# A gated linear attention with a feed-forward block on one core: element work leaves GpSimd, the recurrent state becomes block-diagonal, and the program is put in a new order

## The chip, the core and the metric

The kernel runs on 1 core of one Trainium2 chip. The core has five engines that run their own instruction queues strictly in order and meet only at semaphores: TensorE (PE, matrix multiply, with PEld for its weight loads), VectorE (DVE), ScalarE (ACT), GpSimd (POOL) and SyncE (SP, which here only starts DMAs). The metric is device time in microseconds (us) of the whole program; lower is better. The kernel before takes 174.16 us, the median of 3 runs (172.9 to 175.22).

## The reference: what is computed

```python
batch, n_heads, seq, head_dim = (4, 8, 768, 48)      # r, k, v, w; u is (8, 48)
for t in range(S):
    cur   = einsum('bhd,bhe->bhde', u * k[t], v[t])
    y[t]  = einsum('bhd,bhde->bhe', r[t], state + cur)
    state = w[t][..., None] * state + einsum('bhd,bhe->bhde', k[t], v[t])
x = y.transpose(0, 2, 1, 3).reshape(3072, 384)
out = ((x @ w1) * (x @ w2)) @ w3 @ w_out              # w1, w2: 384 x 1024; w3: 1024 x 1024; w_out: 1024 x 384
```

The first part is a recurrence over 768 steps for 32 pairs of batch and head, with a 48 x 48 state each and a decay w per channel. The second part is a feed-forward block on 3072 tokens.

## The kernel before

**Chunks and units.** The sequence is cut into 6 chunks of 128 steps. Within a chunk the recurrence is done by matrix products: with the running sum of log w over the chunk, r is scaled up and k scaled down, so that the strictly causal part of (r k^T) is one product with a mask, and the state enters once per chunk. A *unit* is one chunk of one or two batches. There are 13 units, numbered 0 to 12: units 0 and 1 have one batch, all others two. In the words below "the ninth unit" is unit 8, and so on.

**The steps of a unit t**, with the names that the program's order uses:
- `win_t`, `kin_t`, `rin_t`, `vin_t`: the loads. All but one are issued by GpSimd. A DMA from GpSimd waits on one of eight semaphores in turn, so that at most eight are under way.
- `ln_t` (ScalarE): log w. `cs_t` (PE): its running sum by a triangular matrix. `ne_t`, `e_t`, `iw_t`, `pc_t` (ScalarE): the exponentials.
- `KRk_t`, `rw_t`, `KRr_t` (VectorE): scaled k and r. `trk_t`, `trr_t` (PE) transpose them through the identity, eight transposes each for a unit of two batches, and `trke_t`, `trre_t` copy them out of PSUM. For units in `DMA_K` and `DMA_R` the DMAs `dtk_t`, `dtr_t` on SP's queue do this instead.
- `m_t_b` (PE): the product r k^T of batch b, 8 heads. `msk_t_b` (VectorE, out of PSUM) applies the causal mask; for the second batch of units 5 to 12 ScalarE copies (`mcp`) and GpSimd applies the mask in place (`maff`).
- `rk_t`, `ruk_t`, `dg_t` (VectorE): the diagonal term with u; `dv_t` multiplies it with v, on GpSimd in nine of 13 units.
- `y_t` (PE): for each head the state times r (L684, a product of 64 rows by 48 columns) and the masked product times v (L690). `yb_t` (VectorE) adds `dv` and writes y.
- `yt_t`, `xT_t`: transposes of y on PE and a copy; for units in `DMA_Y` the DMAs `dty_t_0`, `dty_t_1` on SP's queue.
- `kv_t` (PE), `T_t` (VectorE), `S_t`, `Sb_t`: the new state, its decay and its copy in bf16. `S_t` is on GpSimd in eight units.

**The feed-forward block** of a unit: `a_t_g`, `b_t_g` (PE, L786) are x w1 and x w2, for units of two batches in four groups g of six matmuls each; `asb_t_g` copies a out of PSUM, `abT_t_g` (VectorE, L796) multiplies it with b; `o_t_b` (PE, L802, eight matmuls) is the product with w34; `osb_t_b` copies and `st_t_b` (SP) stores. w34 = w3 w_out is computed once at the start (`wt_`, `w3Te_`, `wm_`, `w34e_`), while the first units run.

**What sets the order.** No scheduler decides. The string `ORDER` lists every step with its engine, `name@engine`, and the program issues the steps in that order; each engine's queue is that list cut down to the engine. `PLACES` gives every step its buffer and its PSUM bank. An entry `warm7@15` issues 15 matmuls on zeros (L373) that keep TensorE busy and compute nothing.

Of the kernel before, what the change touches and what calls it, by code (L numbers as in the profile page):

```python
# [102 lines left out]
et_1@ACT warm1@3 wm_3_0@PE win_2@POOL ne_1@ACT ne_0@ACT wm_6_0@PE ucast@ACT w3_4@POOL wm_7_0@PE warm1@1 wm_7_1@PE
vin_0@POOL wm_2_0@PE w34e_7@DVE vin_1@POOL wm_2_1@PE KRk_1@DVE kin_2@POOL umm@PE KRk_0@DVE trr_1@PE trr_0@PE ucp@ACT
KRr_1@DVE wm_6_1@PE pc_0@ACT w34e_2@ACT rk_1@DVE rin_2@POOL ruk_1@DVE wt_0_0@PE trk_0@PE rk_0@DVE wt_1_0@PE ruk_0@DVE
trk_1@PE w34e_6@DVE wm_3_1@PE win_3@POOL trke_1@ACT KRr_0@DVE wt_1_1@PE trke_0@ACT wt_0_1@PE w3Te_1_0@DVE m_1_0@PE
# [756 lines left out]
```

## Time and profile before

| | |
|---|---|
| median of 3 runs | 174.16 us (172.9 to 175.22) |
| the profiled execution | 173.97 us, its span (first to last instruction) 172.3 us |
| so outside the span | 1.67 us |
| busy share of the span | PE 93%, DVE 77%, ACT 55%, POOL 57% |
| mean granted TensorE clock | 0.988 |
| last matmul ends, and the span after it | 168.2 us, 4.1 us |

A line of the timeline reads: start, length, engine, source line, operation, output and inputs, count, and in brackets how long the engine was idle before it and who released it. In the windows the columns behind the stretch are its length and then the busy time of PE, PEld, DVE, ACT and POOL with the number of instructions, the granted clock, the DMA load and the bytes moved. Times of y_t in what follows are the ends of its last matmuls (L690): y_3 46.95, y_4 60.32, y_5 77.51, y_9 117.16, y_12 145.09 us.

### The profile page before, as it was taken

The numbers are of one execution on the slowest core, as the hardware profiler recorded it, in microseconds if no ns is written. First come the engines' busy times: TensorE is split into PE (matmuls) and PEld (weight loads), VectorE is DVE, ScalarE is ACT, GpSimd is POOL, SyncE is SP. The second block draws the span as 40 slices with busy tenths as digits, with TensorE's granted clock in tenths as the row PEclk, the third lists the DMA queues.
The fourth block names the chain that finished last, engine by engine and source line by source line (L and its number), as shares of the span: only waits on it lengthen the run. The fifth ranks groups of instructions, "written<-read, shape, count | busy, mean of one in ns | idle before, by whom it ended". The sixth has DMA issues, their size and how long they took to land.

```text
span 172.3 us, 4685 instructions
## 1 busy us (share of the span) xinstructions
PE 160.0 (93%) x1956; PEld 119.6 (69%) x1956; DVE 133.2 (77%) x222; ACT 94.1 (55%) x161; POOL 97.8 (57%) x99
## 2 busy tenths in 40 slices
PE   5889999989999999599999999989989899999990
PEld 2364658558897789357778878667767687886750
DVE  4022798989889999969999899997988745856660
ACT  2125387867568699449888769855661430110301
POOL 7975968699988879694599972040057520000000
PEclk9999999999999999969999999999999999999999
DMA  4999999999999999999999999547879803400333
GB/s 70 159 200 171 235 178 189 177 184 163 170 196 175 163 161 197 175 160 205 71 61 234 119 68 157 111 125 158 166 154 111 142 12 83 137 0 4 137 137 139
DMA packets 98663, 24.36 MB, mean 141 GB/s; under 512 B 88833, under 2 KB 97026, under 8 KB 98642
## 3 DMA queue, kind: packets, MB, share of 16 engines
q0 software_dynamic: 81536, 16.06, 107.9%
q1 hardware_dynamic: 17106, 8.00, 18.9%
q8 instruction: 15, 0.25, 0.6%
q14 instruction: 6, 0.05, 0.1%
HBM read 27.79 MB, written 4.72 MB: 189 GB/s over the span
## 4 chain that ended last, share of the span: by engine, by line
PE 54%; DMA 17%; DVE 13%; ACT 5%; POOL 3%; issue 2%; SPq 2%; ACTq 0%; DVEq 0%; POOLq 0%
PE banks L786 25%; PE banks L802 13%; DMA xT<-yb 6%; DMA wo_bf<-in_moe_w_out_dram 6%; DMA win<-in_w_dram 5%; PE banks L437 4%; DVE abT L796 4%; DVE ruk L618 3%; PE banks L647 2%; PE banks L690 2%; PE banks L486 1%; SPq L813 1%; PE banks L744 1%; POOL w_bf L415 1%; DVE rk L598 1%
## 5 line engine op out<-in xcount | busy, mean ns | idle before, releaser
L786 PE MATMUL banks<-xT,w_bf 128*128 128x256 bf16 (+1 forms) x624 | 70.3, 265 | 1.9 <-DMA xT<-yb 1.9
L786 PEld LDWEIGHTS <-w_bf 128*128 128x128 bf16 x624 | 55.9, 98 | 10.4 <-issue 1.9
L796 DVE TENSOR_TENSOR abT<-a_sb,banks 128x512 bf16<-128x512 f32 x48 | 32.1, 680 | 8.8 <-PE banks L786 8.1
L792 ACT COPY a_sb<-banks 128x512 f32<-128x512 f32 x38 | 22.2, 593 | 27.6 <-DVE abT L796 16.0
L802 PE MATMUL banks<-w,abT 128*128 128x384 bf16 x192 | 36.0, 334 | 0.0
L661 POOL TENSOR_SCALAR_AFFINE_SELECT Mbf<-Mbf 128x1024 bf16<-128x1024 bf16 x8 | 8.8, 1096 | 31.5 <-ACT Mbf L653 29.0
L802 PEld LDWEIGHTS <-abT 128*128 128x128 bf16 x192 | 18.3, 99 | 11.2 <-issue 1.0
L666 DVE TENSOR_TENSOR Mbf<-banks,mask 128x1024 bf16<-128x1024 f32 x16 | 19.3, 1216 | 2.3 <-PE banks L647 2.1
L808 ACT COPY osb<-banks 128x384 f32<-128x384 f32 x18 | 8.7, 491 | 20.7 <-PE banks L802 12.4
L389 POOL DMA_DIRECT2D kin<-in_k_dram x13 | 14.6, 1128 | 1.9 <-DVE KK L505 1.2
L389 POOL DMA_DIRECT2D vin<-in_v_dram x13 | 14.8, 1136 | 0.8 <-DMA wo_bf<-in_moe_w_out_dram 0.7
L389 POOL DMA_DIRECT2D rin<-in_r_dram x13 | 14.7, 1135 | 0.2 <-issue 0.2
L389 POOL DMA_DIRECT2D win<-in_w_dram x12 | 13.9, 1156 | 1.5 <-DMA wo_bf<-in_moe_w_out_dram 1.2
L633 POOL TENSOR_TENSOR dv<-vin,dg 128x768 bf16<-128x768 bf16 (+1 forms) x9 | 12.0, 1345 | 4.4 <-DMA vin<-in_v_dram 1.6
L470 ACT ACTIVATE lw<-win 128x768 bf16<-128x768 f32 (+1 forms) x13 | 10.4, 806 | 7.1 <-DMA win<-in_w_dram 7.1
L709 DVE TENSOR_TENSOR yb<-banks,dv 128x768 bf16<-128x768 f32 x10 | 9.5, 954 | 3.8 <-issue 1.7
L437 PE MATMUL banks<-wo_bf,w3T 128*128 128x384 bf16 x64 | 11.9, 326 | 0.3 <-DMA wo_bf<-in_moe_w_out_dram 0.3
L373 PE MATMUL banks<-zeros 128*128 128x512 bf16 x27 | 9.9, 508 | 1.8 <-DVE zeros L288 1.8
L624 DVE TENSOR_REDUCE dg<-ruk 128x16 f32<-128x768 bf16 (+1 forms) x13 | 11.4, 879 | 0.1
L500 ACT ACTIVATE NEt<-banks 128x768 bf16<-128x768 f32 (+1 forms) x13 | 10.0, 778 | 1.5 <-PE banks L491 0.9
L647 PE MATMUL banks<-RT,KT 64*128 64x128 bf16 x192 | 8.7, 218 | 1.9 <-DVE RT L579 1.4
L653 ACT CAST Mbf<-banks 128x1024 bf16<-128x1024 f32 x8 | 8.2, 1020 | 3.9 <-PE banks L647 2.7
(86 smaller groups left out, 232.7 us busy)
## 6 DMA issues: line engine op xcount, KB each, us to landing
out_dram<-osb SPq DMA_DIRECT2D x24, 192.0 KB, 2.1
win<-in_w_dram POOLq DMA_DIRECT2D x11, 384.0 KB, 8.9
kin<-in_k_dram POOLq DMA_DIRECT2D x11, 192.0 KB, 9.3
rin<-in_r_dram POOLq DMA_DIRECT2D x11, 192.0 KB, 9.4
vin<-in_v_dram POOLq DMA_DIRECT2D x11, 192.0 KB, 7.6
w_bf<-in_moe_w_dram POOLq DMA_DIRECT2D x8, 192.0 KB, 7.1
w_bf<-in_moe_w_dram POOLq DMA_DIRECT2D x4, 256.0 KB, 8.5
w_bf<-in_moe_w_dram POOLq DMA_DIRECT2D x2, 512.0 KB, 8.8
```

Of the source, the lines that this page charges most:

```text
L389: QUEUE[eng].dma_start(dst, src)
L437: nc.tensor.matmul(one(f"wm{fi}")[:, :DM], lhsT=x[:, gi, :], rhs=wo_bf[:, gi, :], start=(gi == 0), stop=(gi == FI - 1))
L470: nc.scalar.activation(LW[:, :, :D], ww, Act.Ln)
L500: nc.scalar.activation(dst, cs_view(), Act.Exp, scale=-1.0)
L624: nc.vector.reduce_sum(dgs, ruks, axis=AX.X)
L633: e.tensor_mul(dvs, vv, dgs[:, :, None].to_broadcast([C, bh, D]))
L647: nc.tensor.matmul(o[:, e, q, :], lhsT=KTs[a:a + PAD, b * HP + q, :], rhs=RTs[a:a + PAD, b * HP + q, :], start=True, stop=True)
L666: nc.vector.tensor_mul(Mbf[m].rearrange("s j q t -> s (j q) t"), mview().rearrange("s j q t -> s (j q) t"), mask[:, None, :].to_broadcast( ...
L786: nc.tensor.matmul(o[:, f, :], lhsT=wt[:, di, fi * P:(fi + 1) * P], rhs=x[:, di, :T], start=(di == 0), stop=(di == DI - 1))
L792: copier(eng)(sa, one(f"a{t}_{g}"))
L796: nc.vector.tensor_mul(ab[:, g * per:(g + 1) * per, :T], sa.rearrange("p (f t) -> p f t", t=T), one(f"b{t}_{g}").rearrange("p (f t) -> p f ...
L802: nc.tensor.matmul(one(f"o{t}_{b}")[:, :DM], lhsT=ab[:, fi, b * C:(b + 1) * C], rhs=w34[:, fi, :], start=(fi == 0), stop=(fi == FI - 1))
```

## The change

- **GpSimd** keeps the loads, but of the 25 multiplications and masks it did for the units only six are left: `maff_3_1`, `maff_6_0`, `maff_8_1`, `dv_6`, `dv_7`, `dv_8`. All `S_t` and ten `dv_t` (before: four) are on VectorE.
- **Masks**: each is now either one VectorE product out of PSUM (`mcp_t_b@DVE`, 10 of them; its `maff` then does nothing) or a ScalarE copy and a product in place (14 of them: 11 on VectorE, 3 on GpSimd).
- **Block-diagonal state**: `Sbf` has a zeroed second half, two heads stand on the diagonal of a 128 x 96 block, and `y_t` takes one product of 128 rows by 96 columns for two heads, where it took two of 64 rows by 48. y lies in PSUM in the order of the output. `Sb_t` becomes two copies of 64 partitions, all on ScalarE, and is there for all units with a state (11, before 9).
- **DMA transposes** of k and r also for unit 8, of y also for unit 7: 22 on SP's queue instead of 18.
- **ScalarE's queue** starts the load of w of unit 1.
- **Order**: `ORDER` and `PLACES` are new throughout. Matmuls on zeros: 24 ahead of the first real work or close to it and 2 later, where there were 18 and 9.

ScalarE, around the exponential of unit 3 (`Et`, after which r of unit 3 can be scaled). Before, with `lw<-win_78` being `ln_3` and `lw<-win_80` being `ln_4`:

```order
L470 ACTIVATE lw_83<-win_78 128x16x48
L552 ACTIVATE iw_84<-lw_83 128x768
L442 CAST w_150<-banks 128x384
L500 ACTIVATE NEt_91<-banks 128x768
L470 ACTIVATE lw_83<-win_80 128x16x48
L560 ACTIVATE Et_88<-banks 128x768
```

Now, with `Mbf<-banks` being the copies of two masks of unit 3 and `Sbf<-Sst` the two-part state copies:

```order
L510 ACTIVATE NEt_91<-banks 128x768
L733 COPY xT_129<-banks 128x3x128
L570 ACTIVATE Et_88<-banks 128x768
L710 CAST yb_117<-banks 128x768
L557 ACTIVATE pc_121<-banks 128x8
L452 CAST w_150<-banks 128x384
L791 COPY a_sb_134<-banks 128x512
L604 COPY KT_101<-banks 128x1024
L663 CAST Mbf_105<-banks 128x1024
L663 CAST Mbf_108<-banks 128x1024
L765 CAST Sbf_127<-Sst_125 64x4x48 x2
L480 ACTIVATE lw_82<-win_80 128x16x48
```

`ln_4`, which needs the load of w of unit 4, stood ahead of `e_3` and now stands behind it and, among others, behind two mask copies and a state copy.

GpSimd in the stretch of units 5 to 7. Before (`S_4`, then `dv_5`, then the mask of unit 5):

```order
L759 TENSOR_TENSOR Sst_126<-Tst_124,pc_119 128x384
L389 DMA vin_77<-in_v_dram 128x16x48
L389 DMA win_80<-in_w_dram 128x16x48
L633 TENSOR_TENSOR dv_116<-vin_75,dg_114 128x768
L389 DMA vin_72<-in_v_dram 128x16x48
L661 AFFINE_SELECT Mbf_105<-Mbf_105 128x1024
```

Now, the first two computing steps after `maff_3_1`, which are `maff_6_0` and `dv_6`:

```order
L399 DMA vin_72<-in_v_dram 128x16x48
L678 AFFINE_SELECT Mbf_107<-Mbf_107 128x1024
L399 DMA rin_63<-in_r_dram 128x16x48
L643 TENSOR_TENSOR dv_116<-vin_74,dg_114 128x768
L399 DMA win_79<-in_w_dram 128x16x48
```

`S_4` and `dv_5` have left this queue; both now stand on VectorE.

SP's queue around the transposes of y of unit 9 (`xT_129` before, `xT_131` now; `KT` and `RT` are the transposes of k and r of units 10 and 11, `out_dram` the stores). Before:

```order
L569 DMA_TRANSPOSE RT_103<-RR_97 128x8x128
L813 DMA out_dram<-osb_141 128x384
L584 DMA_TRANSPOSE KT_102<-KK_96 128x8x128
L718 DMA_TRANSPOSE xT_129<-yb_117 128x3x128
L569 DMA_TRANSPOSE RT_104<-RR_97 128x8x128
L813 DMA out_dram<-osb_139 128x384
L813 DMA out_dram<-osb_138 128x384
L718 DMA_TRANSPOSE xT_129<-yb_117 128x3x128
```

Now:

```order
L594 DMA_TRANSPOSE KT_101<-KK_95 128x8x128
L579 DMA_TRANSPOSE RT_103<-RR_98 128x8x128
L719 DMA_TRANSPOSE xT_131<-yb_117 128x3x128 x2
L812 DMA out_dram<-osb_140 128x384
L812 DMA out_dram<-osb_141 128x384
```

The two halves stood apart, with a transpose of r and two stores between them; they now follow each other.

The diff, cut to its core (the two tables are left out but for a line each):

```diff
-DMA_R = {9, 10, 11, 12}
-DMA_K = {9, 10, 11, 12}
-DMA_Y = {8, 9, 10, 11, 12}
+DMA_R = {8, 9, 10, 11, 12}
+DMA_K = {8, 9, 10, 11, 12}
+DMA_Y = {7, 8, 9, 10, 11, 12}
-POOL_MASK = {(5, 1), (6, 1), (7, 1), (8, 1), (9, 1), (10, 1), (11, 1), (12, 1)}
...
-urow@SP table@ACT padr_0@DVE padrr1@DVE padkk0@DVE win_0@SP padet0@DVE w3_1@POOL padkk1@DVE zeros@DVE ones2@DVE
+win_1@ACT win_0@SP padr_2@DVE padlw1@DVE ones2@DVE urow@SP table@ACT w3_1@POOL padkk0@DVE padS1@DVE w3_5@POOL ones@DVE
...
-    Sbf = many(NP, [P, NB * HP, D], BF, "Sbf")
+    Sbf = many(NP, [P, NB * HP, 2, D], BF, "Sbf")
...
+    def multiplier(eng):
+        return nc.gpsimd.tensor_mul if eng == "POOL" else nc.vector.tensor_mul
...
+    for i, x in enumerate(Sbf):
+        @op(f"padS{i}")
+        def _(eng, x=x):
+            nc.vector.memset(x.bitcast(F32), 0.0)
...
+            @op(f"mcp_{t}_{b}")
+            def _(eng, b=b, m=m, mview=mview):
+                if eng == "ACT":
+                    nc.scalar.copy(Mbf[m], mview())
+                    return
+                masked.add((t, b))
+                nc.vector.tensor_mul(Mbf[m].rearrange("s j q t -> s (j q) t"),
+                                     mview().rearrange("s j q t -> s (j q) t"),
+                                     mask[:, None, :].to_broadcast([C, 2 * HP, C]))
+
+            @op(f"maff_{t}_{b}")
+            def _(eng, b=b, m=m):
+                if (t, b) in masked:
+                    return
...
-                        for e in range(2):
-                            a = e * PAD
-                            nc.tensor.matmul(o[:, e, b, q, :], lhsT=RTs[a:a + PAD, b * HP + q, :],
-                                             rhs=Sbf[p][a:a + PAD, (i0 + b) * HP + q, :], start=first[e], stop=False,
-                                             skip_group_check=True)
+                for q in range(HP if c else 0):
+                    nc.tensor.matmul(o[:, b, 2 * q * D:2 * (q + 1) * D], lhsT=RTs[:, b * HP + q, :],
+                                     rhs=Sbf[p][:, (i0 + b) * HP + q, :, :].rearrange("p e d -> p (e d)"),
+                                     start=(q == 0), stop=False, skip_group_check=True)
...
-                elif c < NC - 2:
-                    nc.gpsimd.tensor_mul(Sp, Tp, PCb)
                 else:
-                    nc.gpsimd.tensor_mul(Bp, Tp, PCb)
+                    multiplier(eng)(Sp, Tp, PCb)
...
-                    copier(eng)(Bp, Sp)
+                for e in range(2):
+                    copier(eng)(Bp[e * PAD:(e + 1) * PAD, :, e, :], Sp[e * PAD:(e + 1) * PAD])
```

More of the change, by code (lines that the diff above doesn't have):

```diff
@@ L103 @@
[L103 to L106, printed above, removed]
-mask@POOL w3Te_0_0@ACT dg_0@DVE vin_2@POOL wm_1_0@PE w3Te_0_1@ACT msk_1_0@DVE wm_0_0@PE ln_2@ACT rin_3@POOL wm_0_1@PE
@@ L123 @@
-kin_8@POOL o_2_1@PE T_4@DVE dg_4@DVE a_3_1@PE kin_9@POOL msk_4_0@DVE b_3_1@PE asb_3_1@ACT dv_4@POOL o_0_0@PE iw_5@ACT
-msk_4_1@DVE ln_6@ACT cs_5@PE osb_2_1@DVE win_8@POOL abT_3_1@DVE y_4@PE e_5@ACT rk_5@DVE cs_6@PE rin_7@POOL ne_5@ACT
-yb_4@DVE b_3_3@PE pc_5@ACT iw_6@ACT a_3_2@PE rin_8@POOL ruk_5@DVE osb_0_0@ACT rw_5@DVE yt_4@PE e_6@ACT st_0_0@SP
-a_3_0@PE rw_6@DVE KRk_5@DVE asb_3_2@ACT o_1_0@PE KRr_6@DVE xT_4@ACT kin_7@POOL KRr_5@DVE pc_6@ACT asb_3_0@ACT trr_6@PE
-rk_6@DVE S_4@POOL osb_1_0@ACT trr_5@PE abT_3_3@DVE ne_6@ACT a_4_0@PE st_1_0@SP dg_5@DVE vin_6@POOL trre_6@ACT b_3_2@PE
@@ L128 @@
-KRk_6@DVE trk_5@PE Sb_3@ACT ruk_6@DVE win_10@POOL a_4_3@PE trke_5@ACT trre_5@DVE b_3_0@PE abT_3_2@DVE dv_5@POOL
-asb_4_0@ACT trk_6@PE ln_7@ACT b_4_1@PE trke_6@DVE m_5_1@PE abT_3_0@DVE vin_7@POOL m_5_0@PE mcp_5_1@ACT kv_5@PE
-msk_5_0@DVE o_3_1@PE asb_4_3@ACT maff_5_1@POOL T_5@DVE b_4_3@PE dg_6@DVE osb_3_1@ACT rin_9@POOL ln_8@ACT st_3_1@SP
-m_6_0@PE abT_4_3@DVE y_5@PE iw_8@ACT win_9@POOL msk_6_0@DVE cs_7@PE iw_7@ACT b_4_2@PE vin_8@POOL rk_8@DVE a_4_1@PE
-ne_7@ACT yb_5@DVE o_3_0@PE e_7@ACT kin_12@POOL KRk_7@DVE pc_7@ACT asb_4_1@ACT rk_7@DVE yt_5@PE vin_9@POOL ruk_8@DVE
@@ new lines @@
+iw_3@ACT cs_3@PE dv_2@DVE kv_2@PE ne_3@ACT vin_3@POOL a_0_0@PE S_2@DVE xT_1@ACT yd_2@PE e_3@ACT KRk_3@DVE a_1_0@PE
+w2_2@POOL asb_0_0@DVE yb_2@ACT wm_5_1@PE pc_3@ACT rw_3@DVE yt_2@PE w34e_5@ACT rin_4@POOL trk_3@PE asb_1_0@ACT
+KRr_3@DVE trke_3@ACT xT_2@DVE trr_3@PE w2_3@POOL rk_3@DVE b_2_0@PE trre_3@DVE a_2_0@PE kin_4@POOL ruk_3@DVE m_3_0@PE
+asb_2_0@DVE m_3_1@PE win_5@POOL mcp_3_0@ACT a_2_1@PE abT_2_0@DVE b_0_0@PE mcp_3_1@ACT asb_2_1@DVE b_1_0@PE abT_0_0@DVE
+Sb_1@ACT maff_3_1@POOL a_2_3@PE dg_3@DVE ln_4@ACT b_2_1@PE win_6@POOL Sb_2@ACT abT_1_0@DVE cs_4@PE maff_3_0@DVE
@@ new lines @@
+o_1_0@PE ln_6@ACT KRk_5@DVE dg_4@DVE rin_10@POOL pc_5@ACT trk_5@PE e_5@ACT a_3_3@PE trke_5@DVE iw_6@ACT cs_6@PE
+rw_5@DVE win_8@POOL asb_3_3@ACT kv_4@PE maff_4_1@DVE osb_1_0@ACT a_3_1@PE T_4@DVE ne_6@ACT y_4@PE win_9@POOL dv_4@DVE
+asb_3_1@ACT a_3_0@PE pc_6@ACT S_3@DVE b_3_3@PE yb_4@DVE asb_3_0@ACT kin_11@POOL a_3_2@PE e_6@ACT KRr_5@DVE b_3_0@PE
+ln_7@ACT abT_3_1@DVE kin_7@POOL yt_4@PE S_4@DVE asb_3_2@ACT o_0_0@PE KRk_6@DVE xT_4@ACT abT_3_3@DVE rin_8@POOL
+trr_5@PE rw_6@DVE osb_0_0@ACT a_4_0@PE rk_5@DVE trre_5@ACT st_0_0@SP win_11@POOL abT_3_0@DVE st_2_1@SP trk_6@PE
@@ new lines @@
+asb_4_0@ACT kv_5@PE KRr_6@DVE kv_6@PE trke_6@ACT ruk_5@DVE m_5_1@PE kin_8@POOL m_5_0@PE T_6@DVE b_3_2@PE mcp_5_0@ACT
+mcp_5_1@DVE trr_6@PE vin_7@POOL Sb_3@ACT a_4_2@PE abT_3_2@DVE maff_5_1@DVE b_4_2@PE trre_6@ACT dg_5@DVE b_4_0@PE
+asb_4_2@ACT rk_6@DVE a_4_3@PE kin_12@POOL ln_8@ACT T_5@DVE o_3_1@PE abT_4_0@DVE asb_4_3@ACT maff_5_0@DVE iw_7@ACT
+ruk_6@DVE vin_8@POOL m_6_0@PE osb_3_1@ACT cs_7@PE dv_5@DVE mcp_6_0@ACT y_5@PE abT_4_2@DVE e_7@ACT a_4_1@PE
+maff_6_0@POOL yb_5@DVE b_4_3@PE ne_7@ACT rin_9@POOL dg_6@DVE asb_4_1@ACT m_6_1@PE o_2_0@PE ln_9@ACT KRk_7@DVE
```

243 lines of the change are left out of this document (112 added, 131 removed).

## The prediction

> **What bounds the kernel now.** I read the page's busy shares first, then the chain of waits, then windows cut at the ends of y_4, y_9 and the last matmul.
>
> ```profile
> PE 160.0 (93%) x1956; PEld 119.6 (69%) x1956; DVE 133.2 (77%) x222; ACT 94.1 (55%) x161; POOL 97.8 (57%) x99
> 60.32:117.16 56.84, 54.35 (x756) 42.69 (x752) 53.29 (x79) 44.37 (x75) 37.76 (x34) 0.97 1.55 143
> 117.16:168.19 51.03, 49.57 (x519) 37.57 (x514) 36.83 (x55) 14.51 (x26) 8.92 (x8) 1.00 0.48 103
> ```
>
> TensorE is the bound over the whole: 8.2 us of idle time up to its last matmul at 168.2 (172.3 - 160.0 - 4.1). But between y_4 and y_9 VectorE is busy 53.29 of 56.84 us, nearly as much as TensorE with 54.35. There the two are bounds together, and what delays one delays the other. After y_9 VectorE has room (36.83 of 51.03).
>
> The single largest loss is in that middle stretch. VectorE's, GpSimd's and TensorE's timelines there, with undisturbed instructions of the same shape behind:
>
> ```profile
> 64.27 1.18 DVE L598 TENSOR_TENSOR rk<-rin,kin 128x768 bf16<-128x768 bf16 x1
> 64.98 1.15 POOL L759 TENSOR_TENSOR Sst<-Tst,pc 128x384 f32<-128x384 f32 x1
> 67.30 3.08 DVE L618 TENSOR_TENSOR ruk<-rk,u_bc 128x768 bf16<-128x768 bf16 x1
> 68.46 1.50 POOL L633 TENSOR_TENSOR dv<-vin,dg 128x768 bf16<-128x768 bf16 x1
> 71.03 0.40 PE L647 MATMUL banks<-RT,KT 64*128 64x128 bf16 x8 [1.37 <-DVE RT L579]
> 72.22 0.38 PE L647 MATMUL banks<-RT,KT 64*128 64x128 bf16 x7 [0.39 <-DVE KT L594]
> 73.07 2.74 PE L802 MATMUL banks<-w,abT 128*128 128x384 bf16 x8
> 79.34 1.46 PE L802 MATMUL banks<-w,abT 128*128 128x384 bf16 x8
> 80.75 0.55 DVE L618 TENSOR_TENSOR ruk<-rk,u_bc 128x768 bf16<-128x768 bf16 x1
> 84.22 1.59 DVE L633 TENSOR_TENSOR dv<-vin,dg 128x768 bf16<-128x768 bf16 x1
> 126.00 0.96 DVE L633 TENSOR_TENSOR dv<-vin,dg 128x768 bf16<-128x768 bf16 x1
> ```
>
> ruk_6 took 3.08 us instead of 0.55 and ended when GpSimd's dv_5 ended; rk_6 took 1.18 beside S_4. VectorE's next steps, the transposed r and k, came late, TensorE stood still for 1.37 and 0.39 us, and its next eight matmuls took 2.74 us, not 1.46: half clock. VectorE lost 2.53 + 0.63 us there and 0.63 at dv_6 (1.59 against 0.96), 3.8 us in the stretch.
>
> Two smaller losses: the load of w of unit 4 holds up e_3, and the DMA transposes of y.
>
> ```profile
> 27.89 8.74 DMA win<-in_w_dram
> 36.72 0.85 ACT lw L470
> 33.51:38.51 5.00, 4.21 (x58) 2.71 (x59) 4.34 (x8) 3.66 (x6) 5.00 (x6) 1.00 1.75 179
> 33.51:38.51 5.00, 1.56 (x5) 0.45 (x5) 1.00 1.75 179
> PE banks L786 <- DMA xT<-yb: 1.9, 3, 0.7
> 120.81 1.20 SPq L718 DMA_TRANSPOSE xT<-yb  x1
> 124.54 4.26 DMA xT<-yb
> ```
>
> In the 5 us up to the release TensorE is idle 0.79 us, and 1.56 us of its busy time are five matmuls on zeros (the second row of the window is L373 alone): some 2.0 us are lost when these are counted at 0.24 each. TensorE waits three times for a transposed y, 1.9 us; for unit 9 SP issued one half at 120.81 and the other at 124.54, landing 4.26 us later.
>
> **The change part by part.** The sum is made against the profiled span of 172.3 us, with 1.67 us outside (173.97). Prices are TensorE's pieces on the chain and the groups of VectorE and ScalarE by line and shape:
>
> ```profile
> 92.65 0.45 PE banks L590 x8
> 80.81 0.34 PE banks L728 x6
> 79.50 1.30 PE banks L802 x8
> 91.99 0.66 PE banks L786 x6
> 77.67 0.33 PE banks L486 x2
> 77.99 0.18 PE banks L491 x8
> 85.06 0.31 PE banks L684 x16
> 55.43 0.47 DVE Tst L752
> L594 DVE COPY KT<-banks 128x1024 bf16<-128x1024 bf16 x3 | 2.1, 687 | 0.1
> L653 ACT CAST Mbf<-banks 128x1024 bf16<-128x1024 f32 x8 | 8.2, 1020 | 3.9 <-PE banks L647 2.7 <-PE banks L690 1.1
> L766 ACT CAST Sbf<-Sst 128x384 bf16<-128x384 f32 x6 | 3.2, 536 | 0.0
> ```
>
> *Up to y_4 (60.32 us).* ln_4 now stands behind e_3: the 2.0 us go. The load of k of unit 0 (and of r) is issued ahead of the w_out load; GpSimd's waits show what a load ahead costs:
>
> ```profile
> 14.17 1.17 POOL L389 DMA_DIRECT2D win<-in_w_dram  x1 [1.21 <-DMA wo_bf<-in_moe_w_out_dram]
> 16.77 1.76 POOL L389 DMA_DIRECT2D vin<-in_v_dram  x2 [0.73 <-DMA wo_bf<-in_moe_w_out_dram]
> ```
>
> The second w_out half landed 2.6 us after the first, with one small r load between them; I put 0.7 us on one more such load (ends 0 and 1.3, half of the 2.6). The w of unit 1 goes out on ScalarE's queue, off GpSimd's list. TensorE has one running sum (0.33 + 0.18) and one set of k transposes (0.45) more ahead of y_4, 0.96. While it waits for w_out it now has no matmuls on zeros; the trace shows half clock after waits of 1.37 + 0.39 us, so I put another 1.3 (2.74 - 1.46) there. Together -2.0 + 0.7 + 1.0 + 1.3 = +1.0 us. The Trainium skill, "TensorE: Matmul & The Clock Gate", section "What's actually happening", has the clock halve only after an idle window of about 3.4 us; by that the 1.3 would be nothing and the sum 1.3 less. The row above shows it halved after less than 2 us of gaps, so the trace disagrees and its value is kept.
>
> *y_4 to y_9 (56.84 us).* In the new order this stretch holds on TensorE two b groups, two running sums (one of them without the column products, 0.33), two k transposes, one r and one y transpose set fewer and two o more: -1.32 - 0.84 - 0.90 - 0.45 - 0.34 + 2.60 = -1.25. On VectorE: six S more (0.47 each, the row of T in the same shape; the other end is GpSimd's 1.15), one dv (0.96), three masks in place; five masks out of PSUM stand in both. A mask in place is not in the trace; by ruk's 0.55 for 768 elements it is 0.7, by the mask out of PSUM (1.17, half of 2.34) at most that; I take 0.7. Gone are three copies of k and two of r (0.69 each), one ruk and one rw (0.55 each), one state copy (0.85) and one a copy (0.69). Sum 2.8 + 1.0 + 2.1 - 3.5 - 1.1 - 0.9 - 0.7 = -0.3; the two rows for this:
>
> ```profile
> 56.68 2.34 DVE L666 TENSOR_TENSOR Mbf<-banks,mask 128x1024 bf16<-128x1024 f32 x2
> 105.30 0.85 DVE L766 CAST Sbf<-Sst 128x384 bf16<-128x384 f32 x1
> ```
>
> GpSimd computes 5 things in this stretch where it computed 13, so of VectorE's 3.8 lost us I leave 5/13, 1.5, and take 2.3 off (ends 0 and 3.8). VectorE: 56.84 - 0.3 - 2.3 = 54.2. TensorE: 56.84 - 1.25 - 3.5 (the gaps and the half clock) = 52.1. The larger one counts: -2.6 us.
>
> *y_9 to the last matmul (51.03 us).* Two b and one running sum without columns more, two o fewer: 1.32 + 0.33 - 2.60 = -0.95. The two halves of y_9, y_10 and y_11 are issued with at most one other DMA between them, and before the first use of a new y TensorE has other work of at least 7.1 us (behind y_11: two o, six a or b and the two m of unit 12, 2.6 + 4.0 + 0.5) against some 6.5 us from y to landing (about 1 for yb, 1.2 for the first issue, 4.26 from the second issue on): two of the three waits go, -1.4. Together -2.3. The tail of 4.1 us ends in the same way, copy and store of two blocks: 0.
>
> *The block-diagonal product*: the same columns in half as many matmuls. By L802's 1.30 for 8 x 384 columns, 8 x 96 take 0.33 against the 0.31 of L684's 16: 0 (ends 0 and +0.31 for each of ten units, if the double width cost double time). The zeroing runs on VectorE in the first microseconds, under the waits for loads.
>
> Sum: 172.3 + 1.0 - 2.6 - 2.3 = 168.4, and 1.67 outside: **170.1 us**, 2.3% below 174.16.
>
> **The rivals.**
>
> *VectorE is not relieved* (3.08 had another cause than GpSimd's work, or the six remaining steps cost as much): the change does not do what it says. The middle stretch then keeps its length, +2.6: 172.7 us. For: S, dv and the masks in place, which VectorE takes over, read two tensors from SBUF as rk, ruk and dv do, the three that were stretched, so there are now more that can be hit: five GpSimd steps at up to 2.53 would cost 12.7. Against: both long ones ended beside a GpSimd multiplication, and 13 such steps cost only 3.8. The Trainium skill, "GPSIMD Engine Reference", section "Key points", says that the two engines share SBUF interfaces and collide where VectorE reads two SBUF inputs; it speaks for relief by fewer GpSimd steps and against moving these very steps to VectorE while any are left. The three stretched rows agree with it on the kind of instruction.
>
> *ScalarE becomes the bound, and it gets slower.* Between y_3 and y_5 ScalarE gets two more mask copies (1.02 each), two more `iw`, one `ne`, one `xT` and one o copy:
>
> ```profile
> 46.95:77.51 30.56, 28.61 (x394) 22.98 (x391) 28.52 (x42) 21.51 (x35) 26.31 (x24) 0.94 2.17 175
> L552 ACT ACTIVATE iw<-lw 128x768 bf16<-128x768 bf16 x10 | 8.3, 849 | 0.1
> ```
>
> That is 2.04 + 1.70 + some 2.1 for the last three (by the rows' 0.54 and 0.85), 5.8 us; of two state copies one goes and the other becomes two, 0. If its 9.05 us of idle time there (30.56 - 21.51) are waits that stay, the stretch grows by 5.8 instead of the middle's -2.6: 172.3 + 1.0 + 5.8 - 2.3 + 1.67 = 178.5. It passes the time before (173.97) from 1.3 us of growth on. For: 27.3 us of work (21.51 + 5.8) in some 30. Against: idle time in front of a full queue shrinks.
>
> *TensorE alone bounds*: if w_out comes no later and the clock holds (-2.0 in the first part), and VectorE's idle time shrinks as well, the middle is TensorE's 52.1: 172.3 - 1.0 - 4.7 - 2.3 + 1.67 = 166.0.
>
> **How the numbers follow.** Forecast 0.45, VectorE not relieved 0.22, ScalarE 0.18, TensorE alone 0.15. A measurement of this kernel can tell about 2%: 170.7 and 177.6. The forecast's own range is 167.5 to 172.5 (0.7 and 1.3 of the start, and the ends of VectorE's relief); six tenths of it lie below 170.7. Faster: 0.27 + 0.15 + 0.03 of the first rival = 0.45. Slower: over half of ScalarE's, 0.11, and 0.02 of the rest, 0.13. Same: 0.42. The range of 8 in 10 runs from 165.5 to 178; it leaves out a part of the last rival's lower half and the upper half of ScalarE's.
>
> **What would show it.** On the profile after: no VectorE product of 0.55 us stretched to over 1 us except beside dv_6; y_4 at 60 to 62 us and y_9 some 54 us later; no wait of L786 for xT over 1 us in all; ScalarE's busy share near 63%. The forecast is wrong if TensorE idles for ScalarE's mask copies or a_sb copies between y_3 and y_5, if the first waits for w_out leave it at half clock for longer, or if VectorE waits for the ScalarE half of the masks it now finishes in place.

## The result, and the profile after

The changed kernel took 166.25 us (median of four executions, 165.28 to 171.38) against 174.69 us for the kernel before (172.90 to 176.17); the ratio of the undisturbed executions is 0.953, 95% interval 0.942 to 0.965. It is faster by 4.7%, where the forecast was 170.1 us. Ratios are taken between undisturbed executions, those within 1.5% of the fastest of their kernel in the same round; in the round of b1_dv5, b2_s_dv, b3_ln4 and b5_nopool these are four of the 25 of the kernel before (168.97 to 171.27 us), so that a ratio there comes out higher than its two medians suggest. Single executions of the kernel before lie between 168.97 and 176.17 us in all that follows, with a mean granted clock of 0.975 to 1.000, so differences under some 2 us are read below from the stretches of a profile and not from medians. The fastest executions on record, 168.97 and 165.28 us, lie 2.2% apart.

The profiled execution took 165.28 us, 163.6 of them in the span; it is the fastest of the four. The page of the kernel after, busy times:

```profile
PE 153.5 (94%) x1850; PEld 117.7 (72%) x1851; DVE 129.0 (79%) x229; ACT 110.9 (68%) x191; POOL 76.5 (47%) x79
```

The same three stretches as in the prediction, cut at the ends of y_4 (60.72), y_9 (111.35) and the last matmul (159.35). Columns: length, then busy time and instructions of TensorE, its weight loads, VectorE, ScalarE and GpSimd, then clock, DMA share, GB/s:

```profile
0.00:60.72 60.72, 54.89 (x696) 39.63 (x698) 44.57 (x95) 41.35 (x74) 47.12 (x55) 1.00 1.77 177
60.72:111.35 50.63, 50.63 (x672) 40.48 (x671) 49.56 (x82) 46.40 (x77) 29.41 (x25) 1.00 2.00 182
111.35:159.35 48.00, 48.00 (x486) 37.60 (x484) 34.89 (x54) 22.71 (x40) 0.00 (x0) 1.00 0.43 98
```

From y_4 on TensorE has no gap: its busy time is the length of both stretches. The middle fell from 56.84 to 50.63 us and carries 6.2 of the 8.7 us; the last fell from 51.03 to 48.00; the first grew by 0.4. Some 2.1 of the 6.2 us are the half clock in the profile of the kernel before: at full clock, in almost the same order, the stretch took 54.70 us (b3_ln4 below). And this execution of the kernel after is a good one: in four other profiles of its order (a0_after, a3_dve, a4_act, a5_load) the stretch takes 51.82 to 52.49 us, with 0.8 to 1.5 us of gaps. VectorE's idle time in the middle fell from 3.55 to 1.07 us, and ScalarE, busy 46.40 of 50.63 us, holds nothing up.

VectorE's groups in the middle stretch of the kernel after (line, tile, shape and count, then busy us, mean ns, and idle time before):

```profile
L795 DVE TENSOR_TENSOR abT<-a_sb,banks 128x512 bf16<-128x512 f32 x17 | 11.3, 680 | 0.4 <-PE banks L785 0.2
L666 DVE TENSOR_TENSOR Mbf<-banks,mask 128x1024 bf16<-128x1024 f32 x5 | 6.0, 1217 | 0.2 <-PE banks L657 0.2
L608 DVE TENSOR_TENSOR rk<-rin,kin 128x768 bf16<-128x768 bf16 x7 | 3.8, 548 | 0.0
L628 DVE TENSOR_TENSOR ruk<-rk,u_bc 128x768 bf16<-128x768 bf16 x7 | 3.8, 548 | 0.0
L566 DVE TENSOR_TENSOR rw<-rin,iw 128x768 bf16<-128x768 bf16 x6 | 3.2, 548 | 0.0
```

All seven rk and all seven ruk take 0.55 us, though GpSimd still computes five things here. The timelines of GpSimd and VectorE at two of them:

```profile
74.65 1.09 POOL L678 TENSOR_SCALAR_AFFINE_SELECT Mbf<-Mbf 128x1024 bf16<-128x1024 bf16 x1 [0.73 <-ACT Mbf L663]
76.88 1.49 POOL L643 TENSOR_TENSOR dv<-vin,dg 128x768 bf16<-128x768 bf16 x1
...
74.61 0.96 DVE L712 TENSOR_TENSOR yb<-banks,dv 128x768 bf16<-128x768 f32 x1 [0.16 <-ACT Mbf L663]
76.81 1.22 DVE L666 TENSOR_TENSOR Mbf<-banks,mask 128x1024 bf16<-128x1024 f32 x1
```

Each lies beside a VectorE instruction that reads one operand from PSUM (banks), and that one is no longer than elsewhere. So do the other three (89.94, 94.25 and 98.31 us). TensorE's waits of 0.3 us and more in the kernel after (us in total, times, longest): all lie ahead of y_4, and the transposed y is not among them.

```profile
PE banks L383 <- DVE zeros L293: 2.7, 1, 2.7
PE banks L433 <- DMA w_bf<-in_moe_w_dram: 1.6, 2, 1.4
PE banks L695 <- DMA vin<-in_v_dram: 0.8, 1, 0.8
PE banks L657 <- DVE RT L552: 0.3, 1, 0.3
```

### The profile page after: what moved, and what is told of

It is laid out like the page before. It is cut to its first block, busy times and chain, and to the rows that moved or that the text cites. A ratio compares the mean times of both kernels' runs of the same rounds, so it can differ in the third digit from the quotient of the medians.

```text
span 163.6 us, 4495 instructions
## 1 busy us (share of the span) xinstructions
PE 153.5 (94%) x1850; PEld 117.7 (72%) x1851; DVE 129.0 (79%) x229; ACT 110.9 (68%) x191; POOL 76.5 (47%) x79
## 4 chain that ended last, share of the span: by engine, by line
PE 77%; DMA 17%; issue 1%; POOL 1%; DVE 1%; ACT 0%; ACTq 0%; POOLq 0%
PE banks L785 39%; PE banks L801 19%; DMA vin<-in_v_dram 7%; DMA rin<-in_r_dram 5%; DMA w_bf<-in_moe_w_dram 5%; PE banks L657 3%; PE banks L695 3%; PE banks L496 2%; PE banks L691 2%; PE banks L745 2%; PE banks L600 1%; PE banks L585 1%; PE banks L729 1%; PE banks L501 1%; PE banks L447 1%
## 5 line engine op out<-in xcount | busy, mean ns | idle before, releaser
L795 DVE TENSOR_TENSOR abT<-a_sb,banks 128x512 bf16<-128x512 f32 x48 | 31.9, 681 | 9.8 <-PE banks L785 4.8
L791 ACT COPY a_sb<-banks 128x512 f32<-128x512 f32 x43 | 24.8, 590 | 21.0 <-PE banks L785 16.3
L801 PE MATMUL banks<-w,abT 128*128 128x384 bf16 x192 | 34.7, 326 | 0.0
L663 ACT CAST Mbf<-banks 128x1024 bf16<-128x1024 f32 x14 | 13.9, 1017 | 6.0 <-PE banks L657 5.0
L608 DVE TENSOR_TENSOR rk<-rin,kin 128x768 bf16<-128x768 bf16 (+1 forms) x13 | 6.7, 518 | 10.4 <-DMA rin<-in_r_dram 10.4
L399 POOL DMA_DIRECT2D win<-in_w_dram x11 | 13.0, 1183 | 3.7 <-ACT NEt L510 1.5
L666 DVE TENSOR_TENSOR Mbf<-banks,mask 128x1024 bf16<-128x1024 f32 x10 | 12.1, 1218 | 1.4 <-PE banks L657 1.4
L807 ACT COPY osb<-banks 128x384 f32<-128x384 f32 x20 | 9.8, 489 | 3.3 <-PE banks L801 3.3
L765 ACT CAST Sbf<-Sst 64x384 bf16<-64x384 f32 (+1 forms) x22 | 10.6, 480 | 0.2
L383 PE MATMUL banks<-zeros 128*128 128x512 bf16 x25 | 7.6, 462 | 2.7 <-DVE zeros L293 2.7
L695 PE MATMUL banks<-vin,Mbf 128*128 128x48 bf16 x192 | 8.6, 183 | 0.8 <-DMA vin<-in_v_dram 0.8
```

The costliest lines, as they stand in the source:

```text
L399: QUEUE[eng].dma_start(dst, src)
L663: nc.scalar.copy(Mbf[m], mview())
L666: nc.vector.tensor_mul(Mbf[m].rearrange("s j q t -> s (j q) t"), mview().rearrange("s j q t -> s (j q) t"), mask[:, None, :].to_broadcast( ...
L695: nc.tensor.matmul(o[:, b, h * D:(h + 1) * D], lhsT=Mbf[ms[b]][:, h % 2, h // 2, :], rhs=vv[:, b * H + h, :], start=(c == 0 and h == 0), s ...
L765: copier(eng)(Bp[e * PAD:(e + 1) * PAD, :, e, :], Sp[e * PAD:(e + 1) * PAD])
L791: copier(eng)(sa, one(f"a{t}_{g}"))
```

## Experiments

The theory after the result: the middle stretch is now TensorE's own work, because GpSimd no longer stretches VectorE's products; VectorE's idle time, which the prediction had kept, was slack. The rivals: the new order and the copies taken off VectorE did it, GpSimd's relief being worth little; or VectorE still sets the pace.

**One dv off GpSimd, in the kernel before** (b1_dv5).

```diff
-... abT_3_2@DVE dv_5@POOL asb_4_0@ACT ...
+... abT_3_2@DVE dv_5@DVE asb_4_0@ACT ...
```

> The kernel before with one step moved: dv_5 (the product of v and the diagonal, GpSimd, 1.50 us at 68.46) on VectorE, at its old place in the order. Theory (collision: VectorE's ruk_6 took 3.08 us because GpSimd multiplied beside it): ruk_6 falls to 0.55 to 0.7, dv_5 adds 0.95 on VectorE, the gaps of 1.37 and 0.39 us of TensorE and its half clock behind them go, the stretch from y_4 to y_9 shrinks by 1.5 to 3.4 us and the time with it. Rival (ruk_6 was long for another reason, such as the copies or loads beside it): ruk_6 stays over 2 us and the stretch stays or grows by 0.95.

171.07 us (median of ten) against 173.02; the ratio of undisturbed executions is 1.001 (0.992 to 1.010), so the whole kernel can't be told from before. VectorE's ruk_6, the middle stretch, and TensorE's wait for the transposed y in this kernel:

```profile
67.20 0.54 DVE L618 TENSOR_TENSOR ruk<-rk,u_bc 128x768 bf16<-128x768 bf16 x1
...
60.16:113.15 52.99, 52.48 (x755) 41.88 (x752) 51.77 (x80) 44.37 (x75) 36.57 (x33) 1.00 1.66 154
...
PE banks L786 <- DMA xT<-yb: 2.9, 2, 2.1
```

ruk_6 is back at 0.54, from 3.08, with GpSimd's load issues beside it unchanged: GpSimd's product was the cause. The middle fell by 3.85 us; against a profile of nearly the same order at full clock (54.70, b3_ln4 below) by 1.7. Behind y_9 the waits for the transposed y grew from 1.4 us (0.69 twice) to 2.9, and the last stretch from 51.03 to 52.59: a part was given back there.

**GpSimd's computation left out** (b5_nopool), in the kernel before: 14 names are struck from the order.

```diff
-S_4@POOL S_5@POOL S_6@POOL S_7@POOL S_8@POOL dv_4@POOL dv_5@POOL dv_7@POOL dv_8@POOL
-maff_5_1@POOL maff_6_1@POOL maff_7_1@POOL maff_8_1@POOL maff_9_1@POOL
```

> The kernel before without GpSimd's computation of the middle: S_4 to S_8, dv_4, dv_5, dv_7, dv_8 and the masks maff of units 5 to 9 are left out (the state isn't scaled, the diagonal and the mask are missing there), with everything else as it was. VectorE does exactly the work that it did. Theory (VectorE's stretched products and its waits both came from GpSimd's work): rk_6, ruk_6 and dv_6 fall to 0.55, 0.55 and 0.95, the stretch from y_4 to y_9 falls from 56.84 to 52 to 53 us and VectorE's idle time in it shrinks from 3.55 to under 2.5. Rival of the prediction's middle (the idle time of VectorE stays as it is): 53.0 plus 3.5 of idle time less nothing, that is a gain of 3.8 at the most and VectorE's idle time at 3.5 or more; a gain under 1 would say that GpSimd's computation cost nothing.

169.64 us against 173.02, ratio 0.983 (0.974 to 0.992). The middle stretch:

```profile
60.34:112.70 52.36, 52.21 (x755) 41.94 (x752) 48.76 (x79) 44.13 (x75) 22.62 (x20) 1.00 1.73 156
```

VectorE's 79 instructions take 48.76 us, as many took 53.29 with GpSimd at work: the stretching was 4.5 us, not the 3.8 that the prediction read. Part of the rest is VectorE's state copy (L766, at 105.30 in the kernel before, beside a mask on GpSimd), 0.85 us there and 0.35 here. TensorE has almost no gap left (52.21 of 52.36); VectorE's idle time did stay, at 3.60 us, where I expected under 2.5, but as slack below TensorE. So complete relief, with the work left out and not moved, ends at 52.4 in the old order, at TensorE's work.

**All S and dv on VectorE, old order** (b2_s_dv).

```diff
-                    nc.gpsimd.tensor_mul(Sp, Tp, PCb)
+                    (nc.gpsimd if eng == 'POOL' else nc.vector).tensor_mul(Sp, Tp, PCb)
...
-S_3@POOL ... S_10@POOL dv_4@POOL dv_5@POOL dv_7@POOL dv_8@POOL dv_11@POOL dv_12@POOL
+S_3@DVE ... S_10@DVE dv_4@DVE dv_5@DVE dv_7@DVE dv_8@DVE dv_11@DVE dv_12@DVE
```

> The kernel before with all eight S steps and all dv steps on VectorE, in the old order; GpSimd keeps the eight masks of its half. Nothing is taken off VectorE in exchange (no copies to ScalarE or to the transposing DMA), so this is the relief of GpSimd alone. In the stretch from y_4 to y_9 VectorE gets five S (0.47 to 0.55) and four dv (0.95), some 6.3 us, on 53.3, and loses at most 3.8 of stretching. Theory (collision gone, but VectorE was already nearly full, so the new order's shifting of copies is needed as well): VectorE 55 to 56 us of work, the stretch 56 to 58 us, no change or 1 us slower. Rival (the collision was all that held the stretch): the stretch falls by 2.5 to 4 us.

174.15 us against 173.02, ratio 1.009 (1.005 to 1.013): no gain, as the theory had it.

```profile
60.06:116.26 56.20, 52.94 (x755) 42.00 (x752) 55.02 (x88) 44.34 (x74) 27.59 (x25) 1.00 1.54 144
```

Here VectorE is the bound (55.02 us of work, TensorE 52.94), and it shows what its idle time is then: 1.18 us of 56.20. rk and ruk are back at 0.55 us each. Moving the steps without taking copies off VectorE only fills it.

**Twelve products put back on GpSimd, new order** (a1_pool).

```diff
-S_3@DVE ... S_10@DVE dv_4@DVE dv_5@DVE dv_11@DVE dv_12@DVE
+S_3@POOL ... S_10@POOL dv_4@POOL dv_5@POOL dv_11@POOL dv_12@POOL
```

> The changed kernel with twelve products put back on GpSimd: S_3 to S_10 and dv_4, dv_5, dv_11, dv_12, at their places in the new order; everything else as in the changed kernel. Between y_4 and y_9 GpSimd then computes 12 or 13 things again, as before the change. Theory (GpSimd's steps stretch VectorE's SBUF products and are slower themselves, 1.15 to 1.5 against 0.47 to 0.95, so that the units' chains grow): VectorE's idle time fills again, the stretch grows by 1 to 3 us. Rival (the new order and the copies that went to ScalarE and to the transposing DMA did it, GpSimd's relief is worth little now that TensorE bounds with VectorE some 1 to 2 us below it): growth under 0.7 us.

173.23 us (172.09 to 174.37), beside 173.59 for the kernel before: the whole gain is gone, 7 us where the theory allowed 3. The middle stretch, VectorE's groups in it, and TensorE's waits in this kernel:

```profile
60.36:118.09 57.73, 51.39 (x673) 40.58 (x671) 51.25 (x74) 46.83 (x77) 39.67 (x34) 1.00 1.88 161
...
L795 DVE TENSOR_TENSOR abT<-a_sb,banks 128x512 bf16<-128x512 f32 x17 | 11.2, 677 | 0.1
L608 DVE TENSOR_TENSOR rk<-rin,kin 128x768 bf16<-128x768 bf16 x7 | 6.3, 901 | 0.0
L666 DVE TENSOR_TENSOR Mbf<-banks,mask 128x1024 bf16<-128x1024 f32 x5 | 6.0, 1214 | 0.0
L628 DVE TENSOR_TENSOR ruk<-rk,u_bc 128x768 bf16<-128x768 bf16 x7 | 5.1, 729 | 0.0
L566 DVE TENSOR_TENSOR rw<-rin,iw 128x768 bf16<-128x768 bf16 x6 | 4.3, 729 | 0.0
...
PE banks L657 <- DMA RT<-RR: 2.3, 1, 2.3
PE banks L785 <- DMA xT<-yb: 2.0, 1, 2.0
PE banks L785 <- DVE yb L712: 1.7, 1, 1.7
```

VectorE does eight instructions fewer than in the changed kernel and takes 1.7 us longer. rk, ruk and rw grew by 2.5, 1.3 and 1.1 us; the products that read PSUM (L795, L666) didn't. The second cost is GpSimd's list, which also issues the loads; its timeline and VectorE's at y_4:

```profile
60.34 1.16 POOL L399 DMA_DIRECT2D win<-in_w_dram  x1 [0.63 <-issue]
61.52 1.49 POOL L643 TENSOR_TENSOR dv<-vin,dg 128x768 bf16<-128x768 bf16 x1
...
63.04 0.96 DVE L712 TENSOR_TENSOR yb<-banks,dv 128x768 bf16<-128x768 f32 x1 [3.43 <-POOL dv L643]
```

dv_4 starts when the issue of a load ends, and yb_4 waits 3.43 us for it on VectorE, with TensorE 1.71 behind. VectorE's idle time in the stretch is 6.48 us, from 1.07. The two largest waits of TensorE are for DMA transposes, of y of unit 7 and r of unit 9. That of r was issued 2.75 us later than in the kernel after (101.98, from 99.23), where VectorE is late, but it also took 11.2 us to land, from 6.8. No run shows what made it land so late, so how the 7 us divide between stretching, GpSimd's list and the DMA stays open.

**Work added to one engine of the changed kernel**, beside that kernel itself. Added are repeats of steps in the middle stretch, written with a plus sign:

```diff
+a_4_0@PE a_4_0+@PE ... a_4_3+@PE ... a_5_2+@PE ... a_6_0+@PE     (a2_pe)
+ruk_5@DVE ruk_5+@DVE ... ruk_6+@DVE ... to ruk_9+@DVE             (a3_dve)
+iw_7@ACT iw_7+@ACT ... iw_8+@ACT ... iw_9+@ACT                    (a4_act)
```

> The changed kernel as it is, timed beside the kernels that add work to it: 166 us, ratio 0.95 to 0.96, and the three stretches 60.7, 50.6 and 48.0 us.

> The changed kernel with four sets of six matmuls done twice between y_4 and y_9 (a_4_0, a_4_3, a_5_2, a_6_0; 0.66 us each, 2.6 us of TensorE, nothing else added). Theory (the middle stretch is now TensorE's own work without a gap): the stretch and the time grow by 2.6 us, at least 2.2. Rival (VectorE, with 49.56 of 50.63 us busy, is what sets the pace, and TensorE is full only because its waits don't show): growth under 1.3 us.

> The changed kernel with five products of VectorE done twice between y_4 and y_9 (ruk_5 to ruk_9, 0.55 us each, 2.75 us). VectorE has 1.07 us of idle time in the stretch. Theory (TensorE bounds, VectorE is just below it): VectorE goes to 52.3 us and some idle time, the stretch grows by 1.7 to 2.7 us. Rival (VectorE has room: its steps can drift behind into the last stretch, where it is busy 34.89 of 48.00): growth under 0.8 us.

> The changed kernel with three exponentials of ScalarE done twice between y_4 and y_9 (iw_7, iw_8, iw_9; 0.85 us each, 2.55 us). ScalarE has 4.23 us of idle time in the stretch. Theory (ScalarE's idle time is real room, and queued work uses it up): growth under 0.7 us. Rival (the idle time is waiting that stays, the prediction's case of ScalarE as the bound): growth of 2 to 2.6 us.

Medians and ratios to the kernel before (173.59 in these rounds): unchanged 166.58, 0.960 (0.955 to 0.964); TensorE 171.71, 0.990 (0.985 to 0.994); VectorE 166.81, 0.961 (0.956 to 0.965); ScalarE 166.30, 0.958 (0.954 to 0.962). The middle stretch of the four, in this order:

```profile
60.56:112.47 51.91, 50.83 (x672) 40.40 (x671) 49.69 (x82) 46.48 (x77) 29.43 (x25) 1.00 2.02 179
...
60.45:118.12 57.67, 54.98 (x697) 43.56 (x695) 49.82 (x82) 47.38 (x77) 29.65 (x25) 0.97 1.89 164
...
59.97:111.79 51.82, 51.07 (x673) 40.53 (x671) 51.58 (x87) 46.66 (x77) 29.87 (x25) 1.00 2.02 177
...
61.06:113.27 52.21, 51.08 (x673) 40.58 (x671) 49.65 (x82) 48.95 (x80) 28.97 (x25) 1.00 1.89 174
```

Of the three engines only TensorE makes the kernel longer when it gets more work: it is the bound. VectorE took 1.9 us more and the stretch is as long as in the unchanged kernel, its idle time going from 2.22 to 0.24 us: my expectation for it (1.7 to 2.7 us) was wrong, the rival (room) right. ScalarE's 2.5 us more cost nothing measurable either. On TensorE the 2.6 us cost 5.1 in the median, twice what I expected. In the profile the stretch grew by 5.8, of which 4.15 are busy time (2.64 of matmuls, the rest half clock behind the wait shown here: these 16 matmuls took 1.04 us, 0.62 elsewhere) and the others longer waits for DMA transposes:

```profile
111.86 1.04 PE L657 MATMUL banks<-RT,KT 64*128 64x128 bf16 x16 [2.08 <-DMA RT<-RR]
```

The half clock is not in every execution: one of 171.65 us had a mean clock of 1.000, and what its 5 us are made of is not shown. The DMA transpose of r of unit 9 is where the changed kernel is thin: the unchanged one waits 0.86 us for it in this execution (51.91), and not at all in the first (50.63).

**ln_4 alone behind unit 3's steps, kernel before** (b3_ln4).

```diff
-... yb_2@DVE ln_4@ACT vin_3@POOL ... e_3@ACT cs_4@PE ... trke_3@ACT rk_3@DVE ... a_2_0@PE ...
+... yb_2@DVE vin_3@POOL ... e_3@ACT ... trke_3@ACT ln_4@ACT rk_3@DVE ... a_2_0@PE cs_4@PE ...
```

> The kernel before with ScalarE's ln_4 behind trke_3 instead of ahead of e_3, and TensorE's cs_4 behind a_2_0, so that the wait for the w of unit 4 no longer stands ahead of unit 3. Theory (the prediction's -2.0 us): TensorE's three zero products and the wait go, m_3 comes some 2 us earlier, y_4 ends at 58.3 and the time falls by 2. Rival (other waits stand behind it, such as the loads of w1 and w2 or VectorE's products): less than 0.7 us.

174.19 us against 173.02, ratio 1.015 (1.006 to 1.024). y_4 ended at 61.60, not at 58.3. The product for k of unit 3 in the kernel before, and then, in this one, ScalarE's e_3, VectorE's chain ahead of unit 3's transposes, and TensorE there:

```profile
37.63 0.56 DVE L505 TENSOR_TENSOR KK<-kin,NEt 128x768 bf16<-128x768 bf16 x1 [0.29 <-ACT lw L470]
...
35.86 0.81 ACT L560 ACTIVATE Et<-banks 128x768 bf16<-128x768 f32 x1
...
36.50 0.96 DVE L706 CAST yb<-banks 128x768 bf16<-128x768 f32 x1 [0.27 <-PE banks L700]
37.38 0.55 DVE L556 TENSOR_TENSOR rw<-rin,iw 128x768 bf16<-128x768 bf16 x1
37.84 0.55 DVE L505 TENSOR_TENSOR KK<-kin,NEt 128x768 bf16<-128x768 bf16 x1
...
38.45 0.62 PE L590 MATMUL banks<-I,KK 128*128 128x128 bf16 x8 [0.21 <-DVE KK L505]
40.92 0.48 PE L486 MATMUL banks<-lw,LT 128*128 128x384 bf16 x2 [0.72 <-ACT lw L470]
```

e_3 came 1.6 us earlier (35.86, from 37.47), and TensorE's transposes of k started at 38.45, from 38.35: VectorE, which has yb_2, rw_3 and the product for k to do first, ended at about the same moment as the wait had. In the kernel before it had stood idle for only 0.29 us ahead of that product, so some 0.3 us were to be had there and not 2.0; yb_2 came 0.6 us later in this execution (36.50, from 35.92), so that they did not show either. The rival was right, and cs_4, later now, brought a new wait of 0.72.

**SP's list mended, kernel before** (b4_sp).

```diff
-... dty_8_0@SP ... st_6_1@SP ... dty_8_1@SP ... dty_9_1@SP ... dty_9_0@SP ... dty_10_1@SP ... dty_10_0@SP
+... dty_8_0@SP dty_8_1@SP ... st_6_1@SP ... dty_9_1@SP dty_9_0@SP ... dty_10_1@SP dty_10_0@SP ...
```

> The kernel before with one thing changed in SP's list: the second half of the transposed y of units 8, 9 and 10 is issued directly behind the first (other transposes and stores stood between them). Theory (the prediction's -1.4: the late second half made TensorE wait): the waits for xT between y_9 and the end fall from 1.9 us to 0.5 or less, the last stretch from 51.0 to 49.3 to 49.7 us, the time by 1.4 to 1.9. Rival (the transfers queue on the DMA engines anyway, or another wait stands behind, the transposed r and k of unit 12): under 0.5.

175.45 us (172.89 to 175.91) beside 173.59, and the last stretch 51.52 us. TensorE's largest wait, and ScalarE's copies that it waits for:

```profile
PE banks L786 <- ACT osb L808: 3.1, 2, 1.7
...
115.85 0.48 ACT L808 COPY osb<-banks 128x384 f32<-128x384 f32 x1 [1.67 <-DMA out_dram<-osb]
130.72 0.48 ACT L808 COPY osb<-banks 128x384 f32<-128x384 f32 x1 [2.42 <-DMA out_dram<-osb]
```

This profile has the gaps and the half clock of the kernel before in its middle stretch (57.68 us at a clock of 0.97). No wait for a transposed y is left, but the stores now stand behind transposes that wait for their y, so the four output buffers stay full, ScalarE can't empty PSUM, and TensorE waits for that. Adjacent halves alone gain nothing; the changed order also puts stores ahead of them.

**Products on zeros in the gap, kernel before** (b6_warm).

```diff
-... m_5_1@PE ...
+... warm0@5 m_5_1@PE ...
```

> The kernel before with five products on zeros (0.21 us each, 1.05 us) on TensorE ahead of m_5_1, in the wait of 1.37 us for the transposed r behind the stretched ruk_6. Theory (the wait makes the granted clock fall in many executions, and the fall costs more than the wait): the granted clock is 0.995 to 1.000 in most executions instead of 0.975 to 0.998, and the median falls by 1 to 2 us. Rival (the clock falls elsewhere or for other reasons): the clock spreads as before and the median changes by less than 0.5 us.

173.20 us (172.43 to 173.55) beside 173.59. The first two stretches, and one piece of the first:

```profile
0.00:61.42 61.42, 57.05 (x697) 40.88 (x698) 42.82 (x89) 34.86 (x62) 51.43 (x59) 0.97 1.73 171
61.42:116.03 54.61, 53.73 (x755) 42.51 (x753) 53.07 (x79) 44.30 (x76) 37.46 (x33) 1.00 1.64 149
...
12.48 1.91 PE L423 MATMUL banks<-I,w_bf 128*128 128x128 bf16 x16
```

The middle, at full clock, fell from 56.84 to 54.61 without ruk_6 being touched. But this time the clock fell near 12 us instead (16 transposes in 1.91 us, 1.28 in the profile before), the first stretch grew by 1.1 us, and the time stayed: the rival was right for the whole kernel.

**Loads into free buffers, changed kernel** (a5_load), an attempt at a faster one.

```diff
-vin2=0 kin3=0 win2=1
+vin2=4 kin3=3 win2=3
-... w1_1@POOL ... win_3@POOL ... vin_2@POOL ...
+... vin_2@POOL w1_1@POOL ... win_3@POOL ...
```

> The changed kernel with three loads in buffers that are free (w of unit 2, v of unit 2, k of unit 3), so that GpSimd's list doesn't stop for them (1.54, 1.34 and 1.04 us in the profile after), and with the load of v of unit 2 issued ahead of the second quarter of w1. Theory: y_2 no longer waits 0.76 us for v of unit 2, all that follows comes earlier by 0.5 to 1.2 us, and the kernel takes 165.4 us instead of 166.3. Rival (the DMA engines are busy over 90% there, so that what is issued earlier lands no earlier, or another load comes late in its place): within 0.3 us, or later by as much.

167.04 us (median of six, 166.23 to 167.85), not faster than the 166.25 and 166.58 of the changed kernel. TensorE no longer waits for v of unit 2, y_4 ends at 60.69, and the waits for the transposed r of unit 9 and y of unit 7 are there again (0.95 and 0.50 us), so the rival was right:

```profile
PE banks L657 <- DMA RT<-RR: 0.9, 1, 0.9
PE banks L785 <- DMA xT<-yb: 0.5, 1, 0.5
```

## Why the prediction was right, and where it was not

The direction held, and so did the range over all rivals, 165.5 to 178, with the measured time at its lower end. The forecast itself was 3.9 us too high, and its own range, 167.5 to 172.5, was missed. By its own ledger, against the profile after: first stretch 61.3, was 60.72; middle 54.2, was 50.63; last 48.7, was 48.00; tail 4.1, was 4.25. The middle has 3.6 of the profile's 4.8 us.

**The middle: the step that failed** is "VectorE: 56.84 - 0.3 - 2.3 = 54.2 ... The larger one counts". It kept VectorE's 3.55 us of idle time as if it belonged to VectorE's work, and left 5/13 of the stretching. The idle time was slack: 1.07 us in the profile after, 0.24 with work added (a3_dve), 1.18 where VectorE really is the bound (b2_s_dv). That is 2.5 of the 3.6 us. The other 1.1 are VectorE's work, which fell by 3.7 (53.29 to 49.56) and not by 2.6. All the stretching went, 4.5 us by b5_nopool, where 2.3 were taken off: the remaining five GpSimd steps stretched nothing, and all five fell beside instructions that read PSUM. Without it the work grew by 0.8 (48.76 to 49.56), where -0.3 had been summed.

So TensorE's sum was the larger one: forecast 52.1, measured 50.63 to 52.49 in the five profiles of the new order that have neither more TensorE work nor GpSimd's steps back (the kernel after twice, a3_dve, a4_act, a5_load). Its 3.5 for the gaps and the half clock was too small: by b5_nopool they were 2.5 (56.84 - 54.35) and 2.1 (54.35 - 52.21). The rival "TensorE alone bounds", with 0.15 and 166.0 us, is what happened in the middle. That its number came so near is in part luck: it had the first stretch 1.4 us too short and the middle 1.5 us too long.

**The mechanism was right.** GpSimd's product stretched ruk_6 (3.08 to 0.54 in b1_dv5), and with twelve products back on GpSimd the whole gain is gone (a1_pool, 173.23), by the stretching, GpSimd's list and the late transposes together. The Trainium skill, "GPSIMD Engine Reference", section "1. Specifications", puts the contention on VectorE instructions in a two-port mode or with two SBUF inputs. The groups of a1_pool agree: rk, ruk and rw grew from 548 to 901, 729 and 729 ns, L795 and L666, with one operand from PSUM, were 677 and 1214, from 680 and 1217. The stretched state copy of b5_nopool reads one operand; whether it ran in a two-port mode no run shows.

What the forecast lacked is that relief by moving the steps to VectorE gives nothing in the time by itself (b2_s_dv, 1.009). That the copies which went from VectorE to ScalarE and to the transposing DMA made the room is argued from VectorE's work, 55.02 us there and 49.56 in the kernel after. No run moves the copies alone, and the new order came with them.

**The first stretch** came out near its sum by two errors that cancel. The -2.0 for ln_4 was not there (b3_ln4, in the old order: another chain ended at about the same time). Nor were the +0.7 and +1.3 for a later w_out load and a half clock behind it: in the new order TensorE's first matmul with w_out starts at 15.12 us without a wait. The 1.0 of more work was right: TensorE's matmuls other than those on zeros took 47.3 us, from 46.2. Against it, those on zeros took 7.6, from 9.9, and TensorE's idle time grew from 4.2 to 5.8 us, which the forecast did not have: the wait for the first zeros is 0.9 us longer (2.7, from 1.8), and those for a weight load (1.6) and for v of unit 2 (0.8) are new or longer. Together that is the 0.4.

**The last stretch**: -2.3 forecast, -3.0 measured; both waits for the transposed y in it went (0.69 twice; the third of the 1.9 us, 0.54, lay ahead of y_9), and TensorE's work fell by 1.57 (49.57 to 48.00), not by 0.95. That the halves are issued closely is not enough of a reason (b4_sp); that the stores, too, stand ahead of them is argued from the two orders, not tried alone.

**The block-diagonal product** was priced right; TensorE's rows at y_4 of the kernel after:

```profile
59.80 0.33 PE L691 MATMUL banks<-Sbf,RT 128*128 128x96 bf16 x4
59.97 0.36 PE L695 MATMUL banks<-vin,Mbf 128*128 128x48 bf16 x8
```

The four matmuls of a batch hold TensorE 0.17 us (59.97 - 59.80), 0.34 for a unit, against 0.31.

**The other rivals.** "VectorE is not relieved" (172.7) fell with the first groups after. "ScalarE becomes the bound" (178.5) was wrong: its idle time in the middle is 4.2 us, and another 2.5 us of work went into it at no measurable cost (a4_act). Of the signs named, ScalarE's busy share came out higher (68%, not 63%) and y_9 followed y_4 by 50.6 us, not 54.

## What to carry to other kernels

Where two engines look equally busy, don't add one's idle time to its work: add a few us of harmless work to each in turn, and the engine on which this makes the kernel longer is the bound. A product on GpSimd has three prices, its own time, that of VectorE's SBUF products beside it, and its place behind the load issues in GpSimd's list; and in this kernel moving it to VectorE did not pay until copies left VectorE for it. Before an early wait is removed, look for what else ends at the same moment; before a queue is reordered, for what then stands behind.
